# Threshold attention and a squared-ReLU MLP on one core: the values of the middle steps behind the first turning, the last queries' copy in a visit's first step, and the first weight roundings one to a step

## The chip, the cores and the metric

The kernel runs on one core of a Trainium2 chip. The metric is the device time of one execution in microseconds; of several runs the median counts. Engines are named as in the profile: PE is TensorE's matmul, PEld its loading of weights, DVE is VectorE, ACT is ScalarE, POOL is GpSimd, SP is SyncE, which here only issues transfers.

## The reference

Two blocks follow each other. The first is attention over 8 batches of 8 heads, with 576 positions of width 64, in which only scores within 0.02 of a row's maximum count:

```python
scores = scale * np.matmul(q, k.transpose(0, 1, 3, 2))
thresh = np.max(scores, axis=-1, keepdims=True) - tau
scores = np.where(scores >= thresh, scores, -1000000000.0)
scores = scores - np.max(scores, axis=-1, keepdims=True)
attn = np.exp(scores)
attn = attn / (np.sum(attn, axis=-1, keepdims=True) + 1e-09)
return np.matmul(attn, v).astype(np.float32)
```

Its output, laid out as 4608 tokens of width 512, is the input x of the second block, with weights w_in (512x2048) and w_out (2048x512):

```python
h = x @ w_in
r = np.maximum(h, 0.0)
g = r * r
return (g @ w_out).astype(np.float32)
```

## The kernel before

**Visits and steps.** Two heads make a pair, and the four pairs of a batch give the 512 columns of x for its tokens. A visit is a pair with some of its blocks of 128 queries (blocks 0 to 3; block 4 holds the last 64 queries of both heads together). Visits 0 to 3 take blocks 0 and 1 of the first batch's pairs, visits 4 to 7 blocks 2 to 4 of the same pairs, and from visit 8 on a visit takes whole pairs. One block of one visit is a step. Steps 0 to 10 are written by `early_step`, steps 11 to 39 by the loop at the end of the kernel (the middle steps), later ones by `late_step`. This document speaks of steps by these numbers. In the trace, the scores of step 0 start at 7.37 us, those of step 3 at 21.15, of step 10 at 53.16, of step 11 at 58.35, of step 22 at 125.34 and of step 27 at 155.97.

**What a step does.** `scores` multiplies queries and keys on TensorE into banks 0 to 3 of PSUM (L280; L273 for block 4, whose queries lie in `qmid`). `maxima` takes each row's maximum on VectorE (L317). `exponents` runs on ScalarE (L340, L341, L343; in early steps L331, L332, L335). `threshold` zeroes the small scores and sums on VectorE (L355, L359, L360). `divide` scales on GpSimd (L365, L367). The banks 0 to 3 come free when the threshold has read them, so the scores of the next step follow it.

**Turning and values.** Two steps later `turn` transposes the block's weights on TensorE in three parts (L414, L421 and L427), each into a bank of PSUM, and a copy on ScalarE takes each part to `wT` (L415, L423, L428). Three steps later (in some blocks), `mix` multiplies the turned weights with the values v on TensorE (L530, 20 instructions) into a bank, and a copy on ScalarE takes the result to xT (`put`, L513). In the middle steps turnings and values take their bank from two in turn, numbers 4 and 5: each use of a bank waits until the copy of its previous use has read it. `mixes` says in which step which values are made; of the middle steps these are 13, 16, 19, 22, 24, 26, 27, 29, 31, 32, 34, 36 and 37.

**Last queries.** `split_left` copies the last 64 queries of a pair from `qT` to `qmid` by two small copies on ScalarE (L248). Block 4 of the visit needs them.

**Rounding the weights.** The MLP's weights come in 32 pieces of 128x512. A piece is loaded by SP, then rounded in stages by `round_weights`: stage 0 on ScalarE (L149, L150), stages 1 and 2 on VectorE (L152, L154), stages 3 and 4 on GpSimd (L156, L158). Three raw areas and three working areas are used in turn; `end_rounding` writes stage 4 and issues the load of the piece three later. In early steps, stage 0 stands last on ScalarE before the next step, stages 1 and 2 stand in the next step's `threshold` between L355 and L359, and stages 3 and 4 behind its `divide`. The list `pieces` gives how many pieces begin in each step.

**The MLP.** Once 256 tokens are complete, `add_chunk` puts their pieces of work into a queue. `fill` takes pieces from it, by an estimate of time, at four places in a step. The first chunk's first half is L577, its second half L759; ScalarE and GpSimd follow L577 (L587, L588). `usable` keeps L577 from weights that no earlier step has rounded.

What sets the order on each engine is only the order in which the program is written: every engine works through its own instructions in that order and waits where data or a buffer is missing.

Of the kernel before, what the change touches and what calls it, by code (L numbers as in the profile page):

```python
# [19 lines left out]
def kernel(  # L20
# [15 lines left out]
    HP = H // 2  # L36
# [44 lines left out]
    at = RAW * 2 * WP  # L81
# [292 lines left out]
    def take(what, among):  # L374
        used[what] += 1
        at = among[used[what] % len(among)]
        if what == "mm":
            last_used(at)
        return bank[at]
# [21 lines left out]
    def place_of(n, i):  # L401

        return n % 2 * 4 + 2 * i if n < HP else n % 2 * 5 + 2 * (i - FIRST) if n < 2 * HP else 2 * i

    def turn(vis, i, part):

        w = weights[vis, i][0]
        to = place_of(vis, i)
        ps = take("tx", (4, 5, 6, 7) if early() else (4, 5))
        ps = ps.rearrange("p (c n) -> p c n", n=P)  # L410
        if i < NBLK:
            for n in range(3):
                c = 3 * part + n
                nc.tensor.transpose(ps[:, n, :], w.rearrange("p u k -> p (u k)")[:, c * P:(c + 1) * P], ident)  # L414
            return lambda: nc.scalar.copy(wT[:, to:to + 2, 3 * part:3 * part + 3, :].rearrange("p g c q -> p c g q"),  # L415
                                          ps[:, 0:3, :].rearrange("p c (g q) -> p c g q", g=2))
        elif part < 2:
            rows = slice(part * D, (part + 1) * D)
            for c in range(NBLK):
                at = part * REST + c * P  # L420
                nc.tensor.transpose(ps[:, c, 0:D], w[rows, 0, at:at + P], ident[rows, rows])  # L421
            at = part * (NBLK + 1)
            return lambda: nc.scalar.copy(wT[:, to, at:at + NBLK, :], ps[:, :, 0:D])  # L423
        else:

            for rows, keys in ((slice(0, D), slice(S - REST, S)), (slice(D, P), slice(0, REST))):
                nc.tensor.matmul(ps[rows, 0, 0:D], w[rows, 0, keys], ident[rows, rows], start=True, stop=True)  # L427
            return lambda: nc.scalar.copy(wT[:, to, NBLK, :], ps[:, 0, 0:D])  # L428
# [412 lines left out]
    FIRST = TCH // P  # L841
# [13 lines left out]
    def by_dma(n):  # L855

        return n >= 3 * HP - 1
# [5 lines left out]
    mixes = {}  # L863
# [16 lines left out]
    chunk_at, j = {}, 0  # L880
# [12 lines left out]
    def early():  # L893
        return state["step"] < early_to

    def pieces_of(j):

        todo = [((x // 4 + 1) * NMC, mlp_in, j, x) for x in range(NFT)]
        if j < PLAIN:
            todo += [(n_in + min(f + 1 + f // (NFT - 2), NFT), mlp_out, j, f) for f in range(NFT)]  # L900
        else:
            second = [(n_pieces, product, j, x, half) for x in range(len(PRODUCTS)) for half in range(2)]
            if j < SEVEN:
                return todo + second
            todo, rest = ([(n_pieces, unit, j, *x) for x in part] for part in UNITS)
            todo += second[0:2] + rest + second[2:]
        return todo
# [3 lines left out]
    def add_chunk(j):  # L911
        waiting.extend(pieces_of(j))
        whole.add(j)

    def rate(s):


        if s < out_from:
            return (PIECE_US * sum(x[2] == 0 for x in waiting) + sum(early_values(x) for x in range(s, out_from))) / (out_from - s) - early_values(s)
        have = PIECE_US * len(waiting) - state["left"]  # L920
        best = 1e9
        at = s
        for e in sorted(chunk_at) + [END]:
            if e > s:
                have += sum(other(x) for x in range(at, e))
                at = e
                best = min(best, (have - (RESERVE if e < END else 0)) / (e - s))
                have += PIECE_US * sum(len(pieces_of(x)) for x in chunk_at.get(e, ()))
        return max(best, 0.0) - other(s)

    def early_values(s):

        return EARLY_VALUES_US * (mixes[s][1].stop - mixes[s][1].start) / P if s in mixes else 0.0
# [35 lines left out]
    early_to = min(chunk_at) + 1  # L969
    pieces, left = [], n_pieces  # L970
    for s, (n, i) in enumerate(steps):
        if s < HP * FIRST:
            x = int(n > 0 and i == 1)
        else:
            x = 0 if s == early_to - 1 else 2 if (n, i) in ((HP + 1, FIRST + 1), (2 * HP - 2, FIRST + 1), (2 * HP - 1, FIRST + 1), (2 * HP, FIRST)) else 1
        pieces.append(min(x, left))
        left -= pieces[-1]
    assert left == 0
# [207 lines left out]
    for s in range(END + 1):  # L1186
        state["step"] = s
        if early():
            rounded_by.append(state["rounded"])
            done += pieces[s]  # L1190
            early_step(s)
            continue
        if s >= first_late:
            assert 4 not in kept.values()
            late_step(s)
            continue
        state["usable"] = rounded_by[-1]
        rounded_by.append(state["rounded"])
        on = s < NST
        now = []  # L1200
        if on:
            n, i = steps[s]
            at = visits[n][1].index(i)
            last = at == len(visits[n][1]) - 1
            now = list(range(done, done + pieces[s]))
            done += pieces[s]
            more = n + 1 < len(visits)
            short = n < 2 * HP
            if short and at == 0 and 0 < n + 1 < 2 * HP:
                load_qk(n + 2)  # L1210
            elif not short and at == 1 and not by_dma(n):
                load_qk(n + 1)
            if now:
                round_weights(now[0], 0)
            scores(s)()
            after()
            some_later("gpsimd")
        old = steps[s - 2] if 2 <= s < NST + 2 and not by_dma(steps[s - 2][0]) else None
        at_once = now or old
        lay = on and last and more and not by_dma(n)  # L1220
        if old:
            turn(*old, 0)()
            turn(*old, 1)()
        if on:
            exponents(n, i)
            if s and by_dma(steps[s - 1][0]):
                turn_last(s)
            for p in now[1:]:
                round_weights(p, 0)
            if at == 1:  # L1230
                split_left(n)
            if lay:
                prep(n + 1)
            elif now:
                round_weights(now[0], 1)
        if s in mixes and not old:
            mix(*mixes[s])
            for j in chunk_at.get(s, ()):
                add_chunk(j)
        quarter = rate(s) / 4 if s < END else 1e9  # L1240
        fill(quarter)
        if s in mixes and old:
            mix(*mixes[s])
            for j in chunk_at.get(s, ()):
                add_chunk(j)
        if old:
            turn(*old, 2)()
        state["free"] = s > first_dma
        smooth = s > first_dma + 2 and s not in mixes
        some_later("vector")  # L1250
        some_later("gpsimd")
        if smooth:
            after()
        if on:
            threshold(n, i)
            for fn in prep_at[s] + load_at[s]:
                fn()
            if lay and now:
                round_weights(now[0], 1)
            if now:  # L1260
                round_weights(now[0], 2)
                round_weights(now[0], 3)
            for p in now[1:]:
                assert not lay
                round_weights(p, 1)
                round_weights(p, 2)
                round_weights(p, 3)
            if not at_once:
                divide(n, i)
        if smooth:  # L1270
            fill(quarter)
            after()
            some_later("gpsimd")
        for what in place_at[s]:
            place_blocks(*what)
        some_loads()
        some_later("vector")
        if not smooth:
            some_later("gpsimd")
            fill(quarter)  # L1280
        some_loads()
        if on and at_once:
            divide(n, i)
        fill(quarter)
        some_loads()
        fill(quarter)
        some_loads()
        if on:
            for p in now:
                end_rounding(p)  # L1290
            if at == 0 and 0 < n <= 2 * HP:
                load_v(n)
            elif last and n >= 2 * HP and not by_dma(n):
                load_v(n + 1)
# [35 lines left out]
```

## Time and profile before

| what | us |
|---|---|
| median of 3 runs | 1323.43 (1323.11 to 1323.56) |
| profiled execution | 1322.66 |
| its span, first to last instruction | 1320.9 |
| TensorE busy in the span | 1291.0 |
| VectorE busy | 941.8 |
| GpSimd busy | 785.8 |
| ScalarE busy | 583.8 |

Busy time by stretch, read from the trace in windows of 20 us (20 is the whole window):

| window, us | PE | DVE | ACT | POOL |
|---|---|---|---|---|
| 20 to 40 (early steps) | 19.08 | 16.89 | 14.82 | 10.09 |
| 40 to 60 (early steps) | 17.48 | 17.37 | 17.29 | 15.13 |
| 80 to 100 (middle) | 18.33 | 19.64 | 15.45 | 19.02 |
| 100 to 120 (middle) | 18.35 | 19.58 | 15.50 | 18.84 |
| 140 to 160 (middle) | 18.90 | 16.63 | 14.85 | 18.09 |
| 200 to 220 (middle) | 20.00 | 12.34 | 8.30 | 7.94 |

A busy TensorE here is not TensorE at its peak: the ends of matmuls are modelled. The views used below are the page's shares of the span, the chain of work that ended last (in shares, and in order of time: start, duration, engine, what was written, line, number of instructions), and the timeline (start, duration, engine, line, operation, output and inputs, shape, number, and in brackets the idle time before it and what ended it).

### The profile page before, as it was taken

Reading aid. Unit: us, or ns where it says so; the run is one execution under the profiler, and the core shown is the slowest. Engines: PE = TensorE matmul, PEld = TensorE weight load, DVE = VectorE, ACT = ScalarE, POOL = GpSimd, SP = SyncE. Lnnn points to the kernel's source line nnn. Section 1 sums busy time; section 2 is a strip of 40 time slices with the busy share of each in tenths; the row PEclk is TensorE's granted clock in tenths of the full one; section 3 lists DMA queues with packets and bytes.
Section 4 is the critical chain, followed back from the end, with each engine's and each line's share of the span. In section 5 each row is a group of like instructions: output and inputs, shape, how many; then the busy total and the mean of one; then the engine's idle time right before and its main releaser. Section 6 shows DMA issues by size and latency. Waiting matters only on the chain.

```text
span 1320.9 us, 24730 instructions
## 1 busy us (share of the span) xinstructions
PE 1291.0 (98%) x8862; PEld 1069.3 (81%) x8862; DVE 941.8 (71%) x2026; ACT 583.8 (44%) x1353; POOL 785.8 (59%) x916
## 2 busy tenths in 40 slices
PE   7999999999999999999999999999999999999998
PEld 6666557887887888797878888888887988889997
DVE  6899876787777878788776877878686877622131
ACT  4878773334353526253535343534353434331331
POOL 3799874774747465556564655656574737454351
PEclk9999999999999999999999999999999999999999
DMA  6765531676786878686666768657676866520000
GB/s 128 160 162 144 141 69 62 139 180 163 161 184 165 186 167 203 137 200 163 165 150 165 160 156 188 173 126 185 149 179 138 196 161 164 144 53 9 9 17 17
DMA packets 320907, 185.48 MB, mean 140 GB/s; under 512 B 282224, under 2 KB 282256, under 8 KB 314384
## 3 DMA queue, kind: packets, MB, share of 16 engines
q1 hardware_dynamic: 309120, 115.78, 46.3%
q0 software_dynamic: 10000, 67.92, 12.8%
q8 instruction: 70, 1.15, 0.4%
q14 instruction: 53, 0.43, 0.1%
q10 hardware_dynamic: 1664, 0.21, 0.1%
HBM read 108.04 MB, written 68.42 MB: 134 GB/s over the span
## 4 chain that ended last, share of the span: by engine, by line
PE 84%; DVE 5%; DMA 3%; ACT 2%; POOL 1%; issue 1%; SPq 0%; DVEq 0%; POOLq 0%
PE big L688 29%; PE big L794 28%; PE big L530 10%; PE big L296 8%; PE big L577 4%; PE big L280 2%; PE big L759 2%; DMA wT<-aside 1%; DMA aside<-turned 1%; PE big L414 1%; DVE w L355 1%; DVE st L317 1%; ACT w L343 1%; DVE turned L154 0%; POOL w_in_sb L158 0%
## 5 line engine op out<-in xcount | busy, mean ns | idle before, releaser
L355 DVE SCALAR_TENSOR_TENSOR w<-big,st,w 128x576 f32<-128x576 f32 x269 | 207.8, 807 | 87.2 <-ACT w L343 85.3
L317 DVE TENSOR_REDUCE st<-big 128x1 f32<-128x576 f32 x288 | 204.2, 748 | 83.4 <-PE big L296 61.4
L367 POOL TENSOR_SCALAR w<-w,st 128x576 f32<-128x576 f32 x269 | 243.8, 915 | 29.4 <-DVE st L360 24.7
L794 PE MATMUL big<-wo,gsum 128*128 128x256 f32 x1088 | 243.8, 382 | 0.0
L794 PEld LDWEIGHTS big<-wo,gsum 128*128 128x128 f32 x1088 | 204.4, 190 | 37.0 <-issue 7.6
L688 PE MATMUL big<-xT,w_in_sb 128*128 128x128 f32 x1536 | 187.4, 277 | 1.5 <-DVE g L700 1.4
L688 PEld LDWEIGHTS big<-xT,w_in_sb 128*128 128x128 f32 x1536 | 178.5, 192 | 10.7 <-issue 7.7
L794 PE MATMUL big<-wo,g 128*128 128x256 f32 x816 | 185.3, 382 | 0.1
L343 ACT ACTIVATE w<-big,st 128x576 f32<-128x576 f32 x255 | 174.1, 733 | 0.2 <-issue 0.2
L794 PEld LDWEIGHTS big<-wo,g 128*128 128x128 f32 x816 | 151.6, 190 | 26.1 <-issue 6.5
L530 PE MATMUL big<-wT,vs 128*64 128x320 f32 (+5 forms) x1420 | 159.7, 389 | 6.7 <-DMA wT<-aside 3.3
L530 PEld LDWEIGHTS big<-wT,vs 128*64 128x64 f32 (+1 forms) x1420 | 85.5, 136 | 72.8 <-issue 20.2
L340 ACT ACTIVATE st<-st 128x2 f32<-128x2 f32 (+1 forms) x137 | 27.9, 203 | 256.0 <-DVE st L317 255.0
L365 POOL TENSOR_SCALAR st<-st 128x2 f32<-128x2 f32 (+1 forms) x148 | 35.8, 242 | 176.6 <-DVE w L355 166.0
L436 POOL DMA_DIRECT2D aside<-turned x50 | 29.9, 597 | 177.8 <-DVE turned L465 177.8
L700 DVE TENSOR_TENSOR g<-big,g 128x512 f32<-128x512 f32 x96 | 64.8, 677 | 83.4 <-PE big L688 77.8
L296 PE MATMUL big<-kT,qT 64*128 64x256 f32 (+3 forms) x768 | 107.0, 416 | 0.0
L296 PEld LDWEIGHTS big<-kT,qT 64*128 64x128 f32 x768 | 84.5, 186 | 14.5 <-issue 5.0
L696 ACT ACTIVATE g<-g 128x512 f32<-128x512 f32 x96 | 60.3, 628 | 63.8 <-DVE g L700 63.7
L567 POOL TENSOR_TENSOR gsum<-g 128x512 f32<-128x512 f32 x34 | 46.1, 1355 | 69.8 <-ACT g L697 60.2
L697 ACT ACTIVATE g<-g 128x512 f32<-128x512 f32 x128 | 80.7, 630 | 4.1
L459 DVE STREAM_TRANSPOSE turned<-w 128x512 f32<-128x512 f32 x100 | 70.3, 703 | 0.0
(118 smaller groups left out, 2070.0 us busy)
## 6 DMA issues: line engine op xcount, KB each, us to landing
aside<-turned POOLq DMA_DIRECT2D x50, 1152.0 KB, 4.8
wT<-aside SPq DMA_DIRECT2D x200, 288.0 KB, 5.4
vs<-in_v_dram SPq DMA_DIRECT2D x72, 128.0 KB, 5.8
wo<-in_moe_w_in_dram SPq DMA_DIRECT2D x16, 512.0 KB, 4.8
wo<-in_moe_w_out_dram SPq DMA_DIRECT2D x16, 512.0 KB, 3.6
out_dram<-osb POOLq DMA_DIRECT2D x32, 256.0 KB, 4.2
kl<-in_k_dram SPq DMA_DIRECT2D x113, 72.0 KB, 3.3
ql<-in_q_dram SPq DMA_DIRECT2D x112, 72.0 KB, 5.7
```

The source lines that it names most:

```text
L296: nc.tensor.matmul(big[to, at + x0:at + x1], lhsT, keys[u * D:(u + 1) * D, x0:x1], start=True, stop=True)
L317: nc.vector.tensor_reduce(out=mx[:, u:u + 1], in_=sc[u], axis=AX.XY, op=ALU.max)
L343: nc.scalar.activation(out=w[:, u, :].rearrange("p (h k) -> p h k", h=2), in_=sc[u], func=AF.Exp, bias=bias[:, u:u + 1], scale=SCALE)
L355: nc.vector.scalar_tensor_tensor(out=wu, in0=sc[u], scalar=thr[:, u:u + 1], in1=wu, op0=ALU.is_ge, op1=ALU.mult, accum_out=sm[:, u:u + 1])
L367: nc.gpsimd.tensor_scalar(out=w[:, u, :], in0=w[:, u, :], scalar1=z[:, u:u + 1], scalar2=rcp[:, u:u + 1], op0=ALU.add, op1=ALU.mult)
L459: move(wb[:, 0:h, :, :], whole_[:, 0, :, :, :])
L530: nc.tensor.matmul(ps[u * D:(u + 1) * D, :], vs[n % 2][rows, u * (NBLK + 1) + c, :], wT[rows, at // REST:(at + ps.shape[1]) // REST, NBLK ...
L688: nc.tensor.matmul(to[:, f, :], factor(j, p, q, c)[:, f * P:(f + 1) * P], part[:, c, :], start=(p in "125" and f == 0 and c == 0), stop=(p ...
L696: nc.scalar.activation(out=to, in_=to if src is None else src, func=AF.Relu)
L697: nc.scalar.activation(out=to, in_=to, func=AF.Square)
L700: nc.vector.tensor_tensor(out=x, in0=to, in1=x, op=ALU.add)
L794: nc.tensor.matmul(to, left[:, f, :], wo[:, slot, f, :], start=(f == 0), stop=(f == HF - 1))
```

## The change

Three edits.

First, `pieces`: in the steps before 8, a piece begins in steps 3 to 7 instead of in 3, 5 and 7; from step 8 up to step 10 none begins, where before one each began in steps 8 and 9. By step 11 five have begun in either case.

Second, in the middle steps with values and an old block to turn: the second part of the turning is written after the values instead of before the exponents, and the values before the first `fill` instead of after it. The order on TensorE becomes scores, first part of the turning, values, second part, the first quarter of the MLP's pieces, third part, the rest. Before, it was scores, first part, second part, the first quarter, values, third part, the rest. On ScalarE the order becomes copy of the first part, exponents, copy of the values, copy of the second part, copy of the third; before it was both copies, exponents, copy of the values, copy of the third part.

Third, `split_left` is called in the first step of a middle visit instead of the second, in both cases behind the exponents.

```diff
     for s, (n, i) in enumerate(steps):
         if s < HP * FIRST:
-            x = int(n > 0 and i == 1)
+            x = int(3 <= s < HP * FIRST)
         else:
-            x = 0 if s == early_to - 1 else 2 if (n, i) in ((HP + 1, FIRST + 1), (2 * HP - 2, FIRST + 1), (2 * HP - 1, FIRST + 1), (2 * HP, FIRST)) else 1
+            x = 0 if s < early_to else 2 if (n, i) in ((HP + 1, FIRST + 1), (2 * HP - 2, FIRST + 1), (2 * HP - 1, FIRST + 1), (2 * HP, FIRST)) else 1
...
         if old:
             turn(*old, 0)()
-            turn(*old, 1)()
+            if s not in mixes:
+                turn(*old, 1)()
         if on:
             exponents(n, i)
...
-            if at == 1:
+            if at == 0:
                 split_left(n)
...
-        if s in mixes and not old:
+        if s in mixes:
             mix(*mixes[s])
             for j in chunk_at.get(s, ()):
                 add_chunk(j)
+            if old:
+                turn(*old, 1)()
         quarter = rate(s) / 4 if s < END else 1e9
         fill(quarter)
-        if s in mixes and old:
-            mix(*mixes[s])
-            for j in chunk_at.get(s, ()):
-                add_chunk(j)
         if old:
             turn(*old, 2)()
```

## The prediction

> **What bounds the kernel now.** I read the page first: share of the span, then the chain that ended last.
>
> ```profile
> span 1320.9 us, 24730 instructions
> ...
> PE 1291.0 (98%) x8862; PEld 1069.3 (81%) x8862; DVE 941.8 (71%) x2026; ACT 583.8 (44%) x1353; POOL 785.8 (59%) x916
> ...
> PE 84%; DVE 5%; DMA 3%; ACT 2%; POOL 1%; issue 1%; SPq 0%; DVEq 0%; POOLq 0%
> ```
>
> TensorE sets the end, and its order of work is fixed when the program is written. So time is lost or won where TensorE stands idle or a chain before it grows. The change touches only the first 220 us: the early steps 0 to 10 (7 to 58 us) and the middle steps 11 to 36 (58 to 217 us). From 205 us the chain is TensorE almost without a break, and nothing there waits for an absolute time; a shift at 217 us arrives whole at the end.
>
> *Early steps.* The timeline (start, duration, engine, line), with step 7 first, then step 9, then step 10:
>
> ```profile
> 39.02 2.08 PE L280 MATMUL big<-kT,qT 64*128 64x288 f32 x8
> ...
> 39.73 0.42 DVE L152 TENSOR_SCALAR turned<-turned 128x512 uint32<-128x512 uint32 x1
> ...
> 40.72 0.17 DVE L360 RECIPROCAL st<-st 128x2 f32<-128x2 f32 x1
> 40.80 1.40 DVE L317 TENSOR_REDUCE st<-big 128x1 f32<-128x576 f32 x2
> ...
> 44.02 1.27 POOL L158 TENSOR_TENSOR w_in_sb<-turned 128x512 f32<-128x512 f32 x1
> ...
> 48.90 0.42 DVE L152 TENSOR_SCALAR turned<-turned 128x512 uint32<-128x512 uint32 x1
> ...
> 53.19 1.27 POOL L158 TENSOR_TENSOR w_in_sb<-turned 128x512 f32<-128x512 f32 x1
> ...
> 53.86 0.88 DVE L152 TENSOR_SCALAR turned<-turned 128x512 uint32<-128x512 uint32 x1
> ```
>
> A step is a loop: scores, maxima (L317), exponents, threshold, next scores. The two rounding operations on VectorE (L152, L154) stand between threshold and the next maxima. Alone they take 0.42 us each. At 53.86 L152 takes 0.88: it ends at 54.74, 0.28 us after L158 of the previous piece ends on GpSimd (54.46). The same shows at 58.84, where L154 takes 1.39 beside L158 of 58.60.
>
> *Middle steps.* The chain in order of time, here steps 26 and 27:
>
> ```profile
> 149.62 1.17 PE big L280 x8
> 150.79 0.25 PE big L421 x6
> ...
> 151.06 0.38 ACT wT L423
> ...
> 151.49 2.38 PE big L530 x20
> 153.87 0.26 PE big L427 x4
> 154.13 1.91 PE big L759 x4
> 156.04 1.17 PE big L280 x8
> ```
>
> TensorE stops before the values (L530) for a copy on ScalarE, since values take the bank of the first turning; then it runs through to the next scores. Between 82 and 117 us the chain is instead VectorE and GpSimd (the roundings, L158, then L577 waiting for it).
>
> **The Trainium skill.** "SBUF — State Buffer", section "Who interferes with whom": a `tensor_scalar` of VectorE in a 2-port mode and a GpSimd operation lock one shared port pair, and the one that comes second "fully blocks". The rows above agree: the blocked L152 ends 0.28 us after L158. "PSUM — Partial Sum Buffer", section "Engine vs sequencer instructions": ScalarE's queue is strictly FIFO, and matmuls start in program order. The trace agrees: in step 27 the copy of the values (L513) starts at 160.25, though they were done at 159.06, because the exponents before it end at 160.35.
>
> **Part 1: first roundings, one a step.** Before: first stages in steps 3, 5, 7, 8, 9; after: 3 to 7. Five pieces either way. Each piece's end issues the load of the piece three later on SP (0.4 us to issue, 4.8 to land): that of piece 3 stays in step 4 (33.5, landed by 38.5, read after from about 41), those of pieces 4 to 7 move one or more steps forward on SP, ahead of q, k and v loads that are issued two visits ahead. I cost that at nothing; the cover is those two visits, some 9 us, and without it each load would hold a later one by 0.4. A piece rounded in step s puts two ScalarE operations (L149, L150; 0.71 each) behind the copies of step s, L152/L154 on VectorE into step s+1's threshold, i.e. between scores s+2 and their maxima, and L156/L158 (1.27 each) on GpSimd behind that divide. From scores to scores the steps took: step 3 (no rounding) 4.26; step 4 (ScalarE part only) 4.44; 5 (VectorE part) 4.73; 6, 4.44; 7, 4.74; 8, 4.43; 9 (both, and the copies of the last queries) 4.97; 10 (both, one block, blocked) 5.19.
>
> After, the VectorE part falls into steps 5, 6, 7, 8, 9. In step 7 before, L158 ends at 45.29, that is 6.27 us after its scores (39.02); with a step of 4.74 it reaches 1.53 us into the next one. L152 wants to start 0.7 us into it. It then ends 0.28 after L158, at 1.81 instead of 1.13: 0.69 later, and so do L360, the maxima and the next scores. The step becomes 4.74+0.69=5.43. It stays there: the divide starts 0.69 later and the step is 0.69 longer, so L158 again reaches 1.53 into the next. ScalarE's part hides below that (L150 ends near 2.7, maxima's first result at 3.2). Step 5 has no L158 before it: 4.73, as before. Steps 6 to 9: 4x5.43=21.72 against 4.44+4.74+4.43+4.97=18.58: +3.14. Step 10 loses both roundings: one-block scores 1.24, maxima from about 1.3 to 2.05, and from there as in the trace 2.2 to the next scores: 4.27 against 5.19, -0.92. Sum +2.2 at step 11. If nothing is blocked, it is 4x4.74=18.96: +0.38-0.92=-0.5. These are the two ends; I take +2.2, since the blocked pair is in the trace twice.
>
> **Part 2: step 11 and the steps to 21.** VectorE and GpSimd start step 11 with one piece less (2.0 us of L152/L154 at 58.2 to 60.2, 2.6 us of GpSimd up to 64.2). But steps 11 and 12 end with TensorE's L577 (60.9 to 64.6, 66.8 to 70.5), so this is slack there. In step 13 it counts: values need not wait for the copy (0.49), scores 14 come at 75.95 instead of 76.3, and L158, for which L577 waits at 79.51, is earlier too. -0.4 (between 0 and -1.0). In steps 16 and 19 the 0.66 and 0.64 saved before the values are nothing: the next scores wait for the threshold, and L577 for L158. The copies of the last queries (L248, two of 0.24) move from behind the second to behind the first exponents of a visit; scores 13, 16, 19 waited 0.43, 0.20, 0.20 for them, with VectorE late there anyway; in the first step ScalarE has 0.4 to 0.6 idle. 0.
>
> **Part 3: values behind the first turning.** Twelve steps: 13, 16, 19, 22, 24, 26, 27, 29, 31, 32, 34, 36. Two banks alternate. Before: turning 1 A, turning 2 B, values A, turning 3 B. After: turning 1 A, values B, turning 2 A, turning 3 B. So values wait for nothing, but turning 3 now waits for the copy of the values, which stands in ScalarE's queue behind the exponents (and in step 22 behind a second L149/L150). Behind turning 3 on TensorE are pieces of the second half and the next scores. The step's own order gives:
>
> - Step 26: values start at once after 4 turnings (0.5 us earlier), and end with turning 2 near 153.4; exponents end at 153.92, copy 0.37 (the L248 that stood before it is gone), turning 3 at 154.42 instead of 153.80: +0.62.
> - Step 27: values of one block (0.80) end with turning 2 near 158.8; exponents end at 160.35, copy 0.21, turning 3 at 160.65 instead of 158.99; L759 and scores 28 follow: +1.63, after the 0.03 that scores 28 waited less.
> - Step 22: exponents, then L149/L150 to 131.0, copy to 131.3, turning 3 at 131.41 instead of 130.47: +0.94; maxima 23 (135.07) wait for L154 anyway, but scores 24 follow TensorE.
> - Step 24: waited 0.46 for a copy held by L150; after, -0.31 (turning 3 at 144.0 plus the shift).
> - Step 34: -0.2 (waited 0.24; the copy comes right after the values).
> - Steps 29, 31, 36: four or more L759/L577 stand between turning 2 and turning 3 and cover the copy: 0. Step 32: 0.2, covered by the threshold.
>
> Sum 0.94-0.31+0.62+1.63-0.2=+2.7. If the copy did not hold turning 3, the eight waits before values (0.24 to 0.66) would go instead, of which those in steps 22, 24, 26, 27, 34 lie on the chain: about -1.6.
>
> **Sum.** 2.2-0.4+2.7=+4.5 us. The profiled execution took 1322.66 (span 1320.9 and 1.8 around it): 1327.2; the median of the runs is 0.8 above it, so 1327.9.
>
> **Rivals.** (a) Roundings cost nothing: the lock doesn't compound because L152 gets in first. -0.5-0.4+2.7=+1.8: 1325.2. Against it are the two blocked rows. (b) Turning 3's wait is covered: +2.2-0.4-0.8=+1.0: 1324.4. For it: three of twelve steps are covered; against it, step 27 has nothing between. (c) Faster: the waits before values go (-1.6), turning 3 waits for nothing, and the roundings are free (-0.5-0.4): -2.5, 1320.9. It decides where the copy of the values ends before turning 2 on TensorE; in step 27 it would have to end 1.8 us earlier. (d) Worse: turning 3's lateness makes VectorE's chain late in steps 28, 30 and 33, where scores wait for the threshold, and the SP loads behind it: +8, 1331.4.
>
> **How the numbers follow.** A measurement here tells 0.2% (2.6 us). Forecast 0.64 (its own range 1326 to 1330), (a) 0.16, (b) 0.08, (c) 0.05, (d) 0.07. Slower by over 0.2%: nearly all of the forecast and (d), 0.70. Same: (a), (b) and the forecast's low edge, 0.25. Faster: (c), 0.05. The range reaches down to (b), and up to near (d): 1324.4 to 1331.0.
>
> **What would show it.** Right: L152 of about 1.1 us in steps 6 to 9, those steps 5.4 us; step 10 4.3; TensorE idle 1.8 us before turning 3 in step 27, released by L513, and some 0.9 in 26 and 22; no wait before L530. Wrong: L152 at 0.42 there, or L513 ahead of the exponents' end.

## The result, and the profile after

The changed kernel takes 1326.95 us in the median of 12 runs (1325.38 to 1327.72), against 1323.10 for the kernel before in the runs beside it (1321.53 to 1323.98). The ratio is 1.0030, with a 95% interval of 1.0021 to 1.0038: slower by 3.9 us in the medians. The forecast was 1327.9, or 4.5 us more. The profiled execution took 1326.93, with a span of 1325.1.

First the page of the changed kernel: span, shares, and the chain that ended last by engine.

```profile
span 1325.1 us, 24730 instructions
...
PE 1292.1 (98%) x8862; PEld 1070.6 (81%) x8862; DVE 942.8 (71%) x2026; ACT 584.5 (44%) x1353; POOL 784.8 (59%) x916
...
PE 83%; DVE 5%; DMA 3%; ACT 2%; issue 1%; POOL 1%; SPq 0%; DVEq 0%; POOLq 0%; ACTq 0%
```

The number of instructions is the same, and each engine's busy time moved by no more than 1.3 us. The span grew by 4.2. The work did not grow; the standing still did. Shares of the whole span can't show where, so the steps have to be laid side by side. The table gives the time from the start of one step's scores to the start of the next step's, read from the first score matmul of each step in the two timelines.

| step | before | after | difference |
|---|---|---|---|
| 4 and 5 | 9.17 | 9.18 | 0.0 |
| 6 | 4.44 | 5.42 | +0.98 |
| 7 | 4.74 | 5.36 | +0.62 |
| 8 | 4.43 | 5.42 | +0.99 |
| 9 | 4.97 | 5.47 | +0.50 |
| 10 | 5.19 | 4.26 | -0.93 |
| 11 to 21 | 66.99 | 66.21 | -0.78 |
| 22 | 7.33 | 8.17 | +0.84 |
| 24 | 5.03 | 4.74 | -0.29 |
| 26 | 6.42 | 6.87 | +0.45 |
| 27 | 5.22 | 6.73 | +1.51 |
| 28 | 5.82 | 5.64 | -0.18 |
| 36 | 11.35 | 11.67 | +0.32 |

From the scores of step 3 to those of step 39 the changed kernel takes 219.99 us and the kernel before 215.87: +4.12. Steps 0 to 2 do the same work in all kernels of this study but the last, and the scores of step 3 come anywhere from 20.7 to 22.6 us after the start. So 21.15 before and 21.85 after is taken as a part of that spread and not of the change, and steps are compared below, not the bare spans.

The early steps, in the timeline of the changed kernel, step 8 (start, duration, engine, line, operation, output and inputs):

```profile
46.06 2.10 PE L280 MATMUL big<-kT,qT 64*128 64x288 f32 x8 [0.91 <-DVE wo L355]
46.37 1.27 POOL L158 TENSOR_TENSOR w_in_sb<-turned 128x512 f32<-128x512 f32 x1
46.79 1.13 DVE L152 TENSOR_SCALAR turned<-turned 128x512 uint32<-128x512 uint32 x1
...
47.96 0.43 DVE L154 TENSOR_SCALAR turned<-turned 128x512 uint32<-128x512 uint32 x1
...
48.57 1.40 DVE L317 TENSOR_REDUCE st<-big 128x1 f32<-128x576 f32 x2
```

L158 runs to 47.64 and L152 ends at 47.92, 0.28 later, with a duration of 1.13 instead of 0.42. The maxima begin 2.51 us after the scores instead of 1.78 (in step 7 of the kernel before).

The middle steps, in the view of who waited for whom on TensorE from 60 to 205 us (total, times, longest). First the kernel before:

```profile
PE big L530 <- ACT wT L415: 3.0, 7, 0.7
...
PE big L530 <- ACT wT L423: 0.4, 1, 0.4
```

Then the changed kernel:

```profile
PE big L414 <- ACT xT L513: 5.5, 4, 1.6
...
PE big L427 <- ACT xT L513: 0.5, 1, 0.5
```

The values (L530) wait for no copy any more: 3.4 us in eight waits are gone. In their place the third turning (L414, or L427 for the last queries) waits for the copy of the values (L513): 6.0 us in five waits. Two of them, of 1.48 and 1.46, are in steps 16 and 19 and cost nothing: with the second and third edits (waits of 1.46 each) these steps take 6.78 and 6.94 us, with the third edit alone, which has no such wait, 6.79 and 6.95. Those of steps 22, 26 and 27 (0.94, 0.51 and 1.60) count. The longest is in step 27:

```profile
160.70 0.80 PE L530 MATMUL big<-wT,vs 128*64 128x64 f32 x20
...
161.43 0.55 PE L414 MATMUL big<-ident,wo 128*128 128x128 f32 x3
...
162.07 1.35 ACT L343 ACTIVATE w<-big,st 128x576 f32<-128x576 f32 x2
...
163.32 0.21 ACT L513 COPY xT<-big 128x64 f32<-128x64 f32 x1
...
163.58 0.55 PE L414 MATMUL big<-ident,wo 128*128 128x128 f32 x3 [1.60 <-ACT xT L513]
```

The values are done at 161.50. Their copy starts at 163.32, in the last 0.1 us of the exponents, and takes 0.21; the third turning stands behind it for 1.60 us.

### The profile page after: what moved, and what is told of

Its sections match the earlier page's. It is cut to its first block, busy times and chain, and to the rows that moved or that the text cites. A ratio compares the mean times of both kernels' runs of the same rounds, so it can differ in the third digit from the quotient of the medians.

```text
span 1325.1 us, 24730 instructions
## 1 busy us (share of the span) xinstructions
PE 1292.1 (98%) x8862; PEld 1070.6 (81%) x8862; DVE 942.8 (71%) x2026; ACT 584.5 (44%) x1353; POOL 784.8 (59%) x916
## 4 chain that ended last, share of the span: by engine, by line
PE 83%; DVE 5%; DMA 3%; ACT 2%; issue 1%; POOL 1%; SPq 0%; DVEq 0%; POOLq 0%; ACTq 0%
PE big L688 29%; PE big L794 28%; PE big L530 10%; PE big L296 8%; PE big L577 3%; PE big L759 2%; PE big L280 2%; DMA wT<-aside 1%; DVE st L317 1%; DMA aside<-turned 1%; PE big L414 1%; DVE w L355 1%; ACT w L343 1%; DVE turned L154 1%; PE big L273 0%
## 5 line engine op out<-in xcount | busy, mean ns | idle before, releaser
L367 POOL TENSOR_SCALAR w<-w,st 128x576 f32<-128x576 f32 x269 | 243.1, 912 | 29.7 <-DVE st L360 21.9
L530 PE MATMUL big<-wT,vs 128*64 128x256 f32 (+5 forms) x1420 | 159.5, 389 | 2.9 <-DMA wT<-aside 2.9
L530 PEld LDWEIGHTS big<-wT,vs 128*64 128x64 f32 (+1 forms) x1420 | 85.9, 136 | 66.0 <-issue 21.2
L365 POOL TENSOR_SCALAR st<-st 128x2 f32<-128x2 f32 (+1 forms) x148 | 35.4, 239 | 174.6 <-DVE w L355 163.5
```

The costliest lines, as they stand in the source:

```text
L367: nc.gpsimd.tensor_scalar(out=w[:, u, :], in0=w[:, u, :], scalar1=z[:, u:u + 1], scalar2=rcp[:, u:u + 1], op0=ALU.add, op1=ALU.mult)
L530: nc.tensor.matmul(ps[u * D:(u + 1) * D, :], vs[n % 2][rows, u * (NBLK + 1) + c, :], wT[rows, at // REST:(at + ps.shape[1]) // REST, NBLK ...
```

## The experiments

All are compared step by step with the two kernels, and by time with the kernel before on the same chip.

### Each edit alone

The first edit alone:

```diff
-            x = int(n > 0 and i == 1)
+            x = int(3 <= s < HP * FIRST)
...
-            x = 0 if s == early_to - 1 else 2 if (n, i) in ((HP + 1, FIRST + 1), (2 * HP - 2, FIRST + 1), (2 * HP - 1, FIRST + 1), (2 * HP, FIRST)) else 1
+            x = 0 if s < early_to else 2 if (n, i) in ((HP + 1, FIRST + 1), (2 * HP - 2, FIRST + 1), (2 * HP - 1, FIRST + 1), (2 * HP, FIRST)) else 1
```

> First edit alone: roundings in steps 3 to 7, all else as before. Theory (the lock between L158 and L152 repeats in each step): steps 6 to 9 take 5.4 us each, step 10 takes 4.3, the scores of step 11 come 2.2 us later than before, and some 0.5 of it comes back by step 21; time +1.5 to +2.2 us. Rival (the roundings cost nothing, and the early lateness comes from elsewhere): steps 6 to 9 at 4.7, time -0.5 us. Steps 22, 26 and 27 as before under both: 7.3, 6.4, 5.2.

Measured: 1323.95 against 1322.69, ratio 1.0010 (1.0003 to 1.0016). Steps 6 to 10 took 5.42, 5.37, 5.41, 5.47 and 4.25; steps 22, 26 and 27 took 7.33, 6.43 and 5.21. The scores of step 11 came 2.25 us later after those of step 3 than before, those of step 22 only 1.47, and so it stayed to step 39 (1.44). The early loss and the 0.8 us that come back in steps 11 to 21 both belong to this edit. The return comes in steps 14 (5.76 instead of 5.97) and 16 (5.83 instead of 6.42); steps 11 to 13 take as long as before. The 1.44, and the 1.26 of the medians, fall short of the 1.5 to 2.2 expected, as the return was larger than the 0.5 named.

The second edit alone:

```diff
         if old:
             turn(*old, 0)()
-            turn(*old, 1)()
+            if s not in mixes:
+                turn(*old, 1)()
...
-        if s in mixes and not old:
+        if s in mixes:
             mix(*mixes[s])
             for j in chunk_at.get(s, ()):
                 add_chunk(j)
+            if old:
+                turn(*old, 1)()
         quarter = rate(s) / 4 if s < END else 1e9
         fill(quarter)
-        if s in mixes and old:
-            mix(*mixes[s])
-            for j in chunk_at.get(s, ()):
-                add_chunk(j)
```

> Second edit alone: values behind the first turning, the copy of the last queries still in a visit's second step, roundings as before. Theory (turning 3 waits for the copy of the values behind the exponents): step 22 +0.9, step 26 about +1.0 since L248 now stands before that copy, step 27 +1.5, step 24 -0.3; time +2.5 to +3.5 us. Rival (the wait is covered, and the waits before the values go): time -1.0 to -1.6 us. Steps 3 to 10 as before under both.

Measured: 1326.71 against 1322.69, ratio 1.0029 (1.0018 to 1.0040). Step 22 took 8.16, step 26 7.38 (+0.96), step 27 6.72, step 24 4.74. Steps 4 to 10 were as before within 0.06. From step 3 to step 39: +3.69. Of this, 0.45 was there by step 22, because step 11 took 7.48 in this execution and 6.22 in the others, and the steps up to 21 gave only a part of it back; steps 22 to 36 have +3.24. The medians, at +4.0, lie above the range of 2.5 to 3.5.

The second and third edits, that is the second as above and these lines:

```diff
-            if at == 1:
+            if at == 0:
                 split_left(n)
```

> Second and third edits, without the first. Theory: as the second alone, but step 26 only +0.45, so 0.5 us less than with the second alone; time +2.0 to +2.7 us. Rival (the third edit matters nowhere): the same time as with the second alone.

Measured: 1325.94 against 1322.69, ratio 1.0026 (1.0015 to 1.0037). Step 26 took 6.86 instead of 7.38, and from step 3 to step 39 it is +2.73; the medians, at +3.25, again lie above their range. The third edit is worth 0.5 us in step 26, since there L248 would have stood before the copy for which the third turning waits.

The third edit alone (the same two lines, on the kernel before):

> Third edit alone: the copy of the last queries in a visit's first step. Theory: steps 12, 15 and 18 end 0.2 to 0.4 us earlier, but VectorE and GpSimd are late in the steps that follow and take it back; time within 0.3 us of before. Rival (those waits lie on the path): -0.8 us.

Measured: 1323.18 against 1322.69, ratio 1.0003 (0.9995 to 1.0011). Steps 12, 15, 16, 18 and 19 took 5.76, 5.59, 6.79, 5.59 and 6.95 against 5.96, 5.95, 6.43, 5.97 and 6.55: what these steps gain, later ones lose, and at step 39 the difference is -0.01.

First edit +1.44, second and third +2.73: 4.17 together, where the whole change has +4.12.

### What holds the early steps

In the changed kernel, GpSimd's roundings ahead of its divide:

```diff
-        divide(n, i)
         while rounding:
             p = rounding.popleft()
             round_weights(p, 3)
             end_rounding(p)
+        divide(n, i)
```

> The changed kernel, with GpSimd's two rounding operations (L156, L158) written ahead of the divide in the early steps instead of behind it, so that L158 ends inside its own step. Nothing else moves, the work is the same. Theory (L152 is late because L158 runs): L152 takes about 0.4 to 0.7 us in steps 6 to 9, those steps take 4.7 to 4.9 us instead of 5.4; time 2.0 to 2.7 us under the changed kernel. Rival (the steps are long because ScalarE has L149 and L150 in every one): steps 6 to 9 stay at 5.4, time unchanged.

Measured: 1325.90 against 1322.80, ratio 1.0024 (1.0016 to 1.0032). A miss: steps 6 to 9 took 5.25, 5.24, 5.24 and 5.23, neither 4.8 nor 5.4, and the scores of step 11 came only 0.7 us earlier after those of step 3 than in the changed kernel, where 2.0 to 2.7 were expected. The timeline of this kernel, step 7:

```profile
39.82 2.08 PE L280 MATMUL big<-kT,qT 64*128 64x288 f32 x8 [0.80 <-DVE w L355]
39.86 1.78 POOL L367 TENSOR_SCALAR w<-w,st 128x576 f32<-128x576 f32 x2
40.52 0.43 DVE L152 TENSOR_SCALAR turned<-turned 128x512 uint32<-128x512 uint32 x1
40.99 0.93 DVE L154 TENSOR_SCALAR turned<-turned 128x512 uint32<-128x512 uint32 x1
```

L158 is gone from beside VectorE's roundings, but the divide (L367) now runs there. L152 passes with 0.43, and L154 takes 0.93: it ends at 41.92, 0.28 after the divide (41.64). The block went from one operation to the next, and the 0.50 that L154 lost is the 0.50 by which the step is longer than 4.74. What the expectation missed is that the divide, put last, reaches into the next step just as L158 had. So this run speaks for the lock, but it does not rule out that ScalarE's share would have done something too. For that GpSimd's chain has to be made shorter with ScalarE's and VectorE's work left alone:

```diff
             p = rounding.popleft()
-            round_weights(p, 3)
             end_rounding(p)
```

> The changed kernel without stage 3 of the rounding in the early steps: GpSimd's multiplication L156 is left out for the first five pieces, so their low parts are not scaled, and L158 ends about 1.3 us earlier, before L152 of the next step is ready. ScalarE's and VectorE's work stays. Theory (L152 is late only because L158 runs beside it): L152 takes 0.42 in steps 6 to 9, L154 0.43, the steps take 4.7 to 4.8 us; 2.6 to 3.0 us under the changed kernel up to step 11. Rival (ScalarE's L149 and L150 in every step, or the number of VectorE's operations): steps 6 to 9 stay above 5.2.

Measured: steps 6 to 9 took 4.74, 4.69, 4.71 and 4.75, and the scores of step 11 came 36.79 us after those of step 3, against 39.36 in the changed kernel: 2.57 less, just under the range, since step 3 took 4.46 instead of 4.25 in this execution. Its timeline, step 7:

```profile
40.23 2.08 PE L280 MATMUL big<-kT,qT 64*128 64x288 f32 x8 [0.28 <-DVE w L355]
40.94 0.42 DVE L152 TENSOR_SCALAR turned<-turned 128x512 uint32<-128x512 uint32 x1
41.11 0.32 POOL L365 TENSOR_SCALAR st<-st 128x2 f32<-128x2 f32 x1 [0.70 <-DVE w L355]
...
41.39 0.43 DVE L154 TENSOR_SCALAR turned<-turned 128x512 uint32<-128x512 uint32 x1
```

L149 and L150 still stand in every one of these steps. The rival falls: the steps were long because a GpSimd operation was running when VectorE's rounding was due. The view shows the other direction as well: L365, the first small operation of GpSimd's divide, begins while L152 runs, ends 0.07 us after it and takes 0.32 us, against 0.22 in step 10 of this kernel, where no rounding runs. (The time, 1324.34 against 1322.56, includes the losses in the middle steps.)

### What holds the middle steps

In the changed kernel, one piece of the MLP ahead of the third turning:

```diff
         quarter = rate(s) / 4 if s < END else 1e9
-        fill(quarter)
+        covered = s in mixes and old
+        fill(2 * quarter if covered else quarter)
         if old:
             turn(*old, 2)()
...
-        fill(quarter)
+        if not covered:
+            fill(quarter)
```

> The changed kernel, with one piece of the MLP moved ahead of turning 3 in the steps with values that had one behind it (22, 26, 27, and 36). Same work on TensorE. Theory (TensorE stands still for the copy of the values and for nothing else): step 22 takes 7.2 us instead of 8.2, step 26 6.0 instead of 6.9, step 27 5.2 instead of 6.7; 3.0 to 3.4 us under the changed kernel. Rival (these steps are held by the threshold, or by ScalarE's longer queue): the steps stay within 0.3 of the changed kernel's.

Measured: 1324.51 against 1322.80, ratio 1.0013 (1.0005 to 1.0021). Step 22 took 7.02, step 26 6.29, step 27 5.01; step 24 took 0.07 and step 28 0.39 longer than in the changed kernel; in step 28 the scores now wait part-way for the threshold of step 27 and take 1.63 us instead of 1.24. Step 36, which had no wait behind L513, stayed at 11.67. Sum over steps 22 to 28: -3.0 against the changed kernel, as expected, though step 26 stayed above the 6.0 named. From step 3 to step 39 it is only -2.43: step 3 and step 17 took 0.34 and 1.03 longer in this execution, and steps 18 and 19 gave 0.8 back. The waits of TensorE behind L513 in this kernel, same view and window as above:

```profile
PE big L414 <- ACT xT L513: 2.2, 2, 1.5
```

Of five waits two are left. Those of steps 22, 26 and 27 are gone. The rival falls too: with the same copies on ScalarE the steps become shorter than before the change, as soon as TensorE has something to do.

The old order in three steps only:

```diff
-            if s not in mixes:
+            if s not in mixes or s in (22, 26, 27):
                 turn(*old, 1)()
...
-        if s in mixes:
+        if s in mixes and s not in (22, 26, 27):
             mix(*mixes[s])
...
         fill(quarter)
+        if s in (22, 26, 27):
+            mix(*mixes[s])
+            for j in chunk_at.get(s, ()):
+                add_chunk(j)
```

> The changed kernel, with the old order of turning and values in steps 22, 26 and 27 alone. Theory (only these three lose): they take 7.3, 6.4 and 5.2 us again, 2.6 to 2.9 us under the changed kernel, and all other steps stay as in the changed kernel. Rival (the loss is spread over all steps with values): less than 1.5 us.

Measured: 1324.66 against 1322.80, ratio 1.0010 (1.0004 to 1.0017). Steps 22, 26 and 27 took 7.32, 6.43 and 5.21; over steps 22 to 28 it is 2.62 less than the changed kernel. From step 22 to step 37 it is within 0.1 of the kernel before (96.32 against 96.22), so the other steps with values cost next to nothing in sum: step 24 gains 0.28, and steps 31 and 36 lose 0.15 and 0.33.

### Putting it together

The two edits of GpSimd's order and of the piece, on the changed kernel at once:

> The two edits before together. Theory: they add, 5 to 6 us under the changed kernel and 1 to 2 us under the kernel before, since the waits of TensorE before the values (steps 22, 24, 26, 27, 34) and those of step 13 are gone and nothing has taken their place. Rival: the gain of one is slack of the other, and the time is that of the kernel before.

Measured: 1323.08 against 1322.80, ratio 1.0000 (0.9992 to 1.0008). They add, 3.73 us less than the changed kernel from step 3 to step 39, but the first gave only 0.7 where 2.0 to 2.7 were expected, so the time is that of the kernel before and not less. It agrees with the rival's time for a reason that the rival did not name.

The last run takes from each part what the steps above showed to be worth keeping: few roundings in succession, values behind the first turning where nothing speaks against it, a piece ahead of the third turning in three steps.

```diff
-            x = int(n > 0 and i == 1)
+            x = int(s in (2, 4, 6))
...
-            turn(*old, 1)()
+            if s not in mixes or s in KEPT:
+                turn(*old, 1)()
...
-        if s in mixes and not old:
+        if s in mixes and s not in KEPT:
...
-        fill(quarter)
-        if s in mixes and old:
+        covered = s in (22, 26, 27)
+        fill(2 * quarter if covered else quarter)
+        if s in KEPT:
             mix(*mixes[s])
...
-        fill(quarter)
+        if not covered:
+            fill(quarter)
```

`KEPT` is (29, 31, 32, 36); the diff is against the kernel before, whose roundings in steps 8 and 9 stay. The other lines of the second edit, and the third edit, are as in the change.

> A version put together from the runs before: first roundings in steps 2, 4, 6, 8 and 9 (one pair in succession instead of two before and four after the change), the values behind the first turning in steps 13 to 27 and 34 with one piece ahead of turning 3 in 22, 26 and 27, the old order in 29, 31, 32 and 36, the last queries copied in the first step. Theory (each succession costs 0.7 us, the waits before the values 0.2 to 0.3 each): 1.0 to 1.8 us under the kernel before. Rival (the early gain is slack of steps 11 to 21): the same as the kernel before within 0.4 us.

Measured: 1321.32 (1320.73 to 1323.38) against 1322.56 (1321.56 to 1324.12), ratio 0.9994 (0.9986 to 1.0003). From step 3 to step 39 it is 215.00 against 215.87: -0.87. The steps say that it is faster, by 0.2 us in the early ones and 0.7 in the middle ones; the interval of the times includes no difference, so by the times alone it isn't shown. Steps 4 and 6 took 4.74 and steps 5 and 7 4.43, the reverse of before, since the roundings moved by a step; step 10 is shorter, 4.73 instead of 5.19, and step 8 longer, 4.74 instead of 4.43.

## Why the prediction was right

**Part 1.** Predicted: steps 6 to 9 at 5.43 each and step 10 at 4.27, in sum +2.2 at step 11. Measured: 5.42, 5.36, 5.42, 5.47 and 4.26, in sum +2.16. The reason was right too: L152 took 1.10 to 1.14 in these steps, as computed (0.42 plus 0.69 is 1.11), and went back to 0.42 where no GpSimd operation was under way when it was due. The Trainium skill's statement that of two such operations the second "fully blocks" ("SBUF — State Buffer", "Who interferes with whom") is what the estimate rests on, and the runs agree with it in both directions: a rounding that came second ended 0.28 us after the GpSimd operation, whether that was L158 or the divide, and a small GpSimd operation that came second (L365) was held as well. Two things stay open. L152 takes 0.42 us alone and ends 0.28 after the other, so some 0.14 us of it (an estimate, the difference) are not held up; the 0.28 that the prediction used was measured, not taken from the page. And that L152 runs in a 2-port mode, which the page makes a condition, is seen in no view. Rival (a), that the lock would not compound, is refuted.

**Part 2.** Predicted -0.4, between 0 and -1.0; measured -0.78. The term was sized too small. The prediction put it down to values that need not wait in step 13, and to one piece less in VectorE's and GpSimd's backlog. The run of the first edit alone has -0.78 as well, without any change to the values, and the second and third edits without the first have 0.0 up to step 22. So all of it belongs to the first edit. And it did not come where the prediction put it: with that edit alone, step 13 is unchanged, and steps 14 and 16 give 0.21 and 0.59. The smaller backlog of roundings is the likely reason; how it shortens step 16 was not followed. That the range held the value is in part luck. That the third edit is worth nothing in steps 12 to 19 was right; that it keeps 0.5 us out of step 26 was part of the working and was shown.

**Part 3.** Predicted +0.94, -0.31, +0.62 and +1.63 in steps 22, 24, 26 and 27, and -0.2 in step 34. Measured +0.84, -0.29, +0.45 and +1.51, and -0.07; step 28 gave 0.18 back, as the scores there no longer wait part-way for the threshold (1.24 us instead of 1.42). Place and cause are right in steps 22, 24, 26 and 27. The three losses were put 0.1 to 0.2 too high. In steps 26 and 27 the prediction let the copy start when the exponents end; in the trace it starts 0.1 us before that (step 27: 163.32, with the exponents running to 163.42), and the third turning follows its end after 0.05 us, sooner than the prediction allowed. TensorE's wait in step 26 was 0.51, where some 0.9 was named as a sign. The steps said to be covered were so in step 29 (0.0) and not quite in 31 and 36 (+0.15, +0.32), where the prediction had 0. No wait makes these two longer. Their old block is one of last queries, and the first two parts of its turning are eight short operations (L421). In step 36 they ran as one group and now run as two groups of four with the values between them; first before, then after:

```profile
211.29 0.47 PE L421 MATMUL big<-ident,wo 64*128 64x64 f32 x8
...
215.77 0.41 PE L421 MATMUL big<-ident,wo 64*128 64x64 f32 x4
...
218.42 0.46 PE L421 MATMUL big<-ident,wo 64*128 64x64 f32 x4
```

From the start of such a group to the start of what follows, TensorE took 0.40 us before (L577 starts at 211.69) and takes 0.34 and 0.39 after (L530 at 216.11, L577 at 218.81). That is 0.33 more, which is the whole difference of the step, and the prediction has no term for it. In step 31, where one score matmul stands between the two groups even before, the same count gives 0.15. The run that went back to the old order in these two steps had 6.63 and 11.34 us again.

From step 22 to step 37 the sum is +2.73 where +2.7 was predicted. That it agrees so closely is luck: the five steps named have +2.44 in sum, and what was not foreseen, +0.47 in steps 31 and 36 and -0.18 in step 28, makes up the rest. Rival (b), that the wait is covered, is refuted by step 27; it put 0.8 us on the waits before the values, where the sum above it has 1.6, and gives no reason for the half.

**The sum.** Predicted +4.5; measured +4.12 between steps 3 and 39, and 3.9 in the medians. The difference is the larger return in Part 2. From step 39 to the end all kernels of the study take between 1083.1 and 1083.9 us (span less the start of step 39), in no order that follows their edits, so the shift arrived at the end within that spread, as predicted. Rival (c) fails because no copy of the values ended before the second turning in steps 22, 26 and 27, and (d) because steps 28, 30 and 33, said to be at risk, did not grow.

## What to carry to other kernels

A wait that disappears from an in-order engine has to be followed to the next use of the same buffer: with two banks in turn, freeing the values from one copy tied the third turning to another, which stood behind 1.35 us of exponents. Whether that costs anything is decided by what the in-order engine has written between the two; one piece of work moved there turned a step of 6.7 us into one of 5.0. And work that is free in every second step need not be free in every step: the VectorE operation that found a GpSimd operation running in steps 6 to 9 lost 0.7 us each time, though no engine had more to do.

## What was not expected

Moving GpSimd's operations about did not free VectorE: the block went from L158 to the divide (L154 at 0.93 instead of 0.43), since GpSimd's chain after the threshold, about 4.4 us, nearly fills a step of 4.7, and in both orders one end of it stood under the next rounding.

And some steps were long in one execution and not in that of another kernel with the same work there. Step 17 took 7.39 us in two kernels (a piece ahead of the third turning; the old order in three steps) and 6.35 to 6.37 in the others, and the two steps after it gave most of it back. In these two the traces show a low TensorE clock at that place: in the first, a granted clock of 0.66 and 0.50 of full speed in 97.0 to 99.0 and 99.0 to 100.5 us, where the changed kernel has 1.00 at the same stage; eight score matmuls took 1.69 us instead of 1.24. In the second it is 0.60 and 0.50. The step 11 of 7.48 us with the second edit alone is of the same kind (0.54 and 0.60 from 59 to 63 us, against 1.00 in the kernel before). So single steps have to be compared with the clock beside them; what lowers it for these few microseconds is not shown.
